# A pooled attention with two MLPs on one core: V rounded on GpSimd in the first batch, and new places in the planned order

## The chip, the cores and the metric

The kernel runs on one core of a Trainium2 chip. The core has a matrix engine (TensorE, PE in the rows; PEld is its weight load), VectorE (DVE), ScalarE (ACT), GpSimd (POOL) and SyncE (SP), which issues the DMAs here. The metric is the device time of one execution in microseconds. Three executions of the kernel before took 1319.75, 1320.28 and 1320.74 us; their median, 1320.28 us, is the time before.

## The reference

```python
q_pool = q.reshape(B, H, S // 2, 2, D).mean(axis=3)              # B, H, S, D = 4, 8, 1152, 64
scores = matmul(q_pool, k.transpose(0, 1, 3, 2)) / sqrt(D)
attn   = exp(scores - max(scores)); attn = attn / (sum(attn) + 1e-9)
x      = matmul(attn, v).transpose(0, 2, 1, 3).reshape(2304, 512)
h = x @ moe_w_in;   g = maximum(0.01 * h, h);                  x   = g @ moe_w_out     # 512 -> 2048 -> 512
h = x @ moe2_w_in;  g = where(h > 0, h, exp(min(h, 0)) - 1);   out = g @ moe2_w_out
```

q, k and v arrive in float32, the four weight matrices in float64.

## The kernel before

Every product on TensorE is made of two or three products of numbers that are split in a rounded high half and the rest (the low half). The helper `psplit` makes such a pair: one instruction rounds (a copy to the high half, mostly on ScalarE, L379), a second subtracts (the low half, mostly on GpSimd or VectorE, L386). K and V are split that way once for each head (`prep_k`, `prep_v`, L501 and L561); so are the probabilities after their transpose, and the weights after they have been converted from float64 (`convert`: two ScalarE instructions L411 and L413, two VectorE instructions L415 and L420 and one GpSimd addition L418 for every 256 columns).

The work is cut into 16 pairs of heads (four batches of four pairs). In a pair each of nine tiles of queries goes through the same steps: scores on TensorE (L585), maxima on VectorE (L590, L592), exponentials with row sums on ScalarE (L596), transposes of the probabilities (L637, from the tenth pair on by VectorE and DMA, L613), the split of the transposed tile `pt` (L379, L386), and the product P V (L668). The keys and queries of the second head of a pair are prepared while the first is worked on. When the four pairs of a batch are done, the two MLPs of the batch (up L820, down L854) run while the next batch's attention goes on, so TensorE always has two kinds of work; during the first batch there is no MLP to run. The last batch's MLPs, with the remaining rows of all batches, use a form with fewer products on 384 columns (`mlp_wide`, L1011 and L1073) and run after all attention has ended.

The order is not written by hand. Each step is recorded in `prog` with an engine, a cost and a rank, and `schedule` places the steps on each engine before the program is built: of the steps that are ready the one of lowest rank goes first. Ranks count in tiles (nine to a pair), and the table PLAN gives batch, layer, first rank, length in ranks and form of each MLP. LS, LR and LE are how many ranks ahead of its tile a step stands (scores, maxima, exponentials), PVLAG how many behind (P V), PREP where the second head's keys and queries stand against the pair. PATIENCE is the share of its own cost for which a step is held back when one of much lower rank is about to be ready; HOLD (in ns) is how long GpSimd holds back while VectorE, still busy, has a step waiting that uses the memory port shared by the two. On the chip every engine works off its own list in order and waits for what an instruction needs.

Of the kernel before, what the change touches and what calls it, by code (L numbers as in the profile page):

```python
# [9 lines left out]
F32 = mybir.dt.float32  # L10
# [37 lines left out]

class Program:

    PATIENCE = 0.5
    GAP = 16
    HOLD = 500
    HELD = 0
    BANKS = 8
    LATENCY = {"PE": 200, "SP": 3000, "DVE": 130, "DVE POOL": 200, "ACT": 155, "ACT POOL": 170, "POOL": 150,
# [195 lines left out]
def kernel(  # L252
# [26 lines left out]
    NP = H // 2  # L279
# [19 lines left out]
    WAHEAD = 1  # L299
    ACB = DC  # L300
    XFB = 5
    WH = "ACT"
    WL = "POOL"
    GH = "ACT"
    GL = "POOL"
# [17 lines left out]
    CAPS = (dict(s=4, t=4, o=1, h=2), dict(s=3, t=2, o=1, h=3), dict(s=3, t=2, o=1, h=7))  # L323
    T1B = 3
    WLAG = 1
    PLAN = ((0, 0, 34.0, 23.0, 0), (0, 1, 57.0, 23.0, 0), (1, 0, 80.0, 15.64, 0), (1, 1, 95.64, 15.64, 0), (2, 0, 111.28, 18.36, 0), (2, 1, 129.64, 18.36, 0), (3, 0, 148.0, 24.0, 1), (3, 1, 172.0, 24.0, 1))
    PBUF = 7
    DTB = 9
    DTC = (0, 1, 2)
    DTE = ("POOL", "POOL", "POOL")  # L330
    DTR = 0
# [2 lines left out]
    KKL = 0.5  # L334
    KH = 'ACT'
    ORDER = (0, 1, 2)
    LS = 2.5
    LR = 2
    LE = 0.3
    PVLAG = 0.5  # L340
    PREP = -1.5

    const = ctx.enter_context(tc.tile_pool(name="const", bufs=1))
    ident = const.tile([128, 128], F32, name="ident")
# [81 lines left out]
    def load_w(rank, layer, w_in, w_out, f, mine):  # L426

        src = (w_in[:, f * 128:(f + 1) * 128].rearrange("(c p) f -> p c f", p=128),
               w_out[f * 128:(f + 1) * 128, :])
        wi = mine("wi", [128, 2, DC, 128], F32R, WIB, "qT", KTB)  # L430
        wo = mine("wo", [128, 2, DM], F32R, WOB, "kT", KTB)
        both = lambda w: w.ap.rearrange("p a c n -> p (a c n)" if w is wi else "p a n -> p (a n)")
        flat = (lambda a: wi[:, a].rearrange("p c n -> p (c n)"), lambda a: wo[:, a])
        r = None
        for i, w in enumerate((wi, wo)):
            if (layer, f, i) in kept:
                kp = kept[layer, f, i]
                prog.add("SP", Move(128, 4096), rank - WAHEAD, lambda w=w, kp=kp: nc.sync.dma_start(
                    out=f32(both(w)), in_=kp.ap), w=[w], r=[kp])
                continue  # L440
            if r is None:
                r = sb("wr", [128, 1024], F32, WRB)
            o = 512 * i
            if w_in.dtype == F32:
                view = lambda o=o, i=i: r[:, o:o + 512].rearrange("p (c n) -> p c n", c=1 if i else DC)
                prog.add("SP", Move(128 if i else 512, 2048 if i else 512), rank - 1.5,
                         lambda i=i, view=view: nc.sync.dma_start(
                             out=view(), in_=src[i] if i == 0 else src[i].rearrange("p (c n) -> p c n", c=1)),
                         w=[(r, o), (r, o + 256)])
            else:  # L450
                convert(rank - CLEAD, r, src[i], o)
            psplit(rank - 0.5, WH, WL, lambda i=i: flat[i](0), lambda i=i: flat[i](1),
                   lambda o=o: r[:, o:o + 512], 512, (w, 0), [(r, o), (r, o + 256)], (w, 1))
            kp = kept[layer, f, i] = Buf(lambda i=i: dram.tile([128, 1024], F32, name=f"w{layer}_{f}_{i}"))
            prog.add("SP", Move(128, 4096), rank, lambda w=w, kp=kp: nc.sync.dma_start(
                out=kp.ap, in_=f32(both(w))), w=[kp], r=[w])
        return wi, wo
# [43 lines left out]
    def prep_k(rank, b, hp, j):  # L501
        kr = raw[b, hp, j, "k"]
        kn = sb("kn", [128, KC, 2 * D], F32R)
        psplit(rank, KH, "POOL", lambda: kn[:, :, 0:D], lambda: kn[:, :, D:2 * D], lambda: kr.ap,
               KC * D, (kn, "h"), [kr], fast=False)
        kT = sb("kT", [128, KC * 128], F32R, KTB)
        for c in range(3):
            t = tr_r(rank, kn, lambda i, c=c: kn[:, 3 * c + i, :], 3, [kT])
            prog.add("ACT", act(384), rank, lambda t=t, c=c: A.activation(  # L509
                out=kT[:, 384 * c:384 * c + 384].rearrange("p (c n) -> p c n", c=3),  # L510
                in_=f32(t[:, 0:3, :]), func=ACTF.Copy), w=[(kT, c)], r=[t])
        prep[b, hp, j, "k"] = kT
# [48 lines left out]
    def prep_v(rank, b, hp, j):  # L561
        vr = raw[b, hp, j, "v"]
        vn = sb("vn", [128, KC, 2 * D], F32R, KTB)
        o = D * j
        psplit(rank, KH, "POOL", lambda: vn[:, :, o:o + D], lambda: vn[:, :, D - o:2 * D - o],
               lambda: vr.ap, KC * D, (vn, "h"), [vr], fast=False)
        prep[b, hp, j, "v"] = vn

# [31 lines left out]
        return p  # L600

    def by_dma(b, hp):
        return b * NP + hp >= DTB

    def split_p(rank, b, hp, j, g, half, p, pt, c0):

        cs = DTC if by_dma(b, hp) else ()
        transpose_p(rank, p, [(pt, c0, 0, 128)], [c for c in ORDER if c not in cs], by_dma(b, hp))
        for c in cs:
            if not half:  # L610
                turned[j, g, c] = sb("wr", [128, 4, 3, 2, 32], F32, WRB, 1)
            tb = turned[j, g, c]
            prog.add("DVE", dve(384) + 60, rank, lambda c=c, tb=tb: V.transpose(  # L613
                out=tb[:, :, :, half, :].rearrange("p j k q -> p k j q"), in_=p[c].ap), w=[(tb, half)], r=[p[c]])
        if not half:
            return
        for c in cs:
            tb = turned[j, g, c]
            d = Buf(lambda c=c: dram.tile([4, 32, 4, 192], F32, name=f"p{b}_{hp}_{j}_{g}_{c}"))
            for i in range(4):  # L620
                prog.add("SP", Move(128, 768, 600), rank + DTR, lambda d=d, i=i, tb=tb: nc.sync.dma_start(
                    out=d.ap.rearrange("j a i r -> i a j r")[i],
                    in_=tb[32 * i:32 * i + 32].rearrange("a j k t q -> a j (k t q)")), w=[(d, i)], r=[tb])
            prog.add("SP", Move(128, 3072), rank + DTR, lambda c=c, d=d: nc.sync.dma_start(
                out=f32(pt[c][:, 1, 0:4]).rearrange("p i k r -> p (i k r)"),
                in_=d.ap.rearrange("j a i r -> (j a) (i r)")), w=[(pt[c], "d")], r=[d])
            psplit(rank + DTL, "ACT", DTE[c], lambda c=c: pt[c][:, 0, 0:4], lambda c=c: pt[c][:, 1, 0:4],
                   lambda c=c: f32(pt[c][:, 1, 0:4]), 3 * 256, (pt[c], ("h", 0)),
                   [(pt[c], "d")], (pt[c], ("l", 0)), fast=False)
# [145 lines left out]
    def mlp(at, span, blocks, layer, w_in, w_out, wide):  # L775
# [31 lines left out]
        def up(f):  # L807
# [5 lines left out]
            for hf, n in enumerate(cuts):  # L813
                h = hbank()
                t = mine("t1", [128, MAIN], F32, T1B, "raw", RAWB)
                tn, hn = lambda t=t, n=n: t[:, 0:n], lambda h=h, n=n: h[:, 0:n]

                def mm(h, c, n, hf):
                    for a, e in ((0, 0), (0, 1), (1, 0)):
                        PE.matmul(  # L820
                            out=h[:, 0:n], lhsT=wi[:, a, c, :], rhs=xs[hf][c][:, e],
                            start=(c == 0 and a == 0 and e == 0), stop=(c == DC - 1 and a == 1))

                for c in range(DC):
                    prog.add("PE", 3 * mmc(n), rank + step * hf / 2, lambda h=h, c=c, n=n, hf=hf: mm(h, c, n, hf),
                             w=[h], r=[wi, xs[hf][c]], want=[g[f][hf], t])
                rk = rank + step * hf / 2 - HURRY
                if layer == 0:
                    prog.add("ACT", act(n), rk, lambda tn=tn, hn=hn: A.activation(
                        out=tn(), in_=hn(), func=ACTF.Copy, scale=0.01), w=[t], r=[h])  # L830
                    prog.add("DVE", dve(n), rk, lambda tn=tn, hn=hn: V.tensor_tensor(
                        out=tn(), in0=hn(), in1=tn(), op=ALU.max), w=[t], r=[h, t])
                else:
                    prog.add("ACT", act(n), rk, lambda tn=tn, hn=hn: A.activation(
                        out=tn(), in_=hn(), func=ACTF.Exp), w=[t], r=[h])
                    prog.add("ACT", act(n, sbuf=True), rk, lambda tn=tn: A.activation(
                        out=tn(), in_=tn(), func=ACTF.Relu, bias=1.0, scale=-1.0), w=[t], r=[t])
                    prog.add("DVE", dve(n), rk, lambda tn=tn, hn=hn: V.scalar_tensor_tensor(  # L838
                        out=tn(), in0=tn(), scalar=-1.0, in1=hn(), op0=ALU.mult, op1=ALU.max),
                        w=[t], r=[h, t])  # L840
                psplit(rk, GH, GL, lambda gf=g[f][hf]: gf[:, 0], lambda gf=g[f][hf]: gf[:, 1], tn, n,
                       (g[f][hf], 0), [t], (g[f][hf], 1))

        def down(fc):
# [320 lines left out]
```

## Time and profile before

| | |
|---|---|
| median of three executions | 1320.28 us |
| the profiled execution, its time | 1319.28 us |
| its span, first to last instruction | 1317.2 us |
| busy: PE, DVE, ACT, POOL | 1272.9, 986.1, 925.6, 717.9 us |
| share of the span: PE, DVE, ACT, POOL | 97%, 75%, 70%, 55% |
| granted TensorE clock, mean | 0.999 |
| the chain that ended last | PE 78%, DVE 9%, ACT 8%, POOL 2%, DMA 2% |

The time of the profiled execution is 2.1 us longer than its span. The shares are means over three stretches that differ: attention alone (the first 150 us or so), attention beside MLPs (to about 1040 us), and the two wide MLPs. Matmuls overlap in the rows, so a TensorE that is shown busy may still run its matmuls further apart than they need to be.

### The profile page before, as it was taken

How to read it: one execution, taken by the hardware profiler on the slowest of the kernel's cores; microseconds unless marked ns; L12 is line 12 of the kernel's file. 1: busy time of each engine (PE TensorE's matmuls, PEld its weight loads, DVE VectorE, ACT ScalarE, POOL GpSimd, SP SyncE). 2: the span in 40 equal slices, each digit the busy share in tenths (PEclk: the TensorE clock that was granted, in tenths of full speed). 3: DMA queues.
4: the chain of work that ended last, by engine and by line, in shares of the span. 5: the costliest groups of instructions: out<-in, count | busy, mean ns of one | idle time of the engine just before them, and what ended most of it. 6: DMA issues, size and time to landing. Idle time of an engine off the chain costs nothing.

```text
span 1317.2 us, 22381 instructions
## 1 busy us (share of the span) xinstructions
PE 1272.9 (97%) x7016; PEld 1113.0 (84%) x7016; DVE 986.1 (75%) x2211; ACT 925.6 (70%) x2385; POOL 717.9 (55%) x633
## 2 busy tenths in 40 slices
PE   6998999999999999999999999999999999999998
PEld 5777878888878888888888888888888799998897
DVE  6999887888888989565665666666755677788876
ACT  8999989999899998665667666766675432226542
POOL 5344336776677765655566555665554464433530
PEclk9999999999999999999999999999999999999999
DMA  6343425666656657998898979988988444443331
GB/s 189 117 152 124 148 65 187 208 224 207 216 197 234 224 203 252 328 286 291 258 301 283 307 242 320 318 286 289 284 272 275 170 145 138 135 144 113 136 119 49
DMA packets 145653, 277.78 MB, mean 211 GB/s; under 512 B 15744, under 2 KB 77184, under 8 KB 145536
## 3 DMA queue, kind: packets, MB, share of 16 engines
q1 hardware_dynamic: 145536, 276.36, 64.2%
q8 instruction: 56, 0.92, 0.3%
q14 instruction: 61, 0.50, 0.1%
HBM read 195.56 MB, written 71.30 MB: 203 GB/s over the span
## 4 chain that ended last, share of the span: by engine, by line
PE 78%; DVE 9%; ACT 8%; POOL 2%; DMA 2%; issue 1%; SPq 0%; DVEq 0%; POOLq 0%; ACTq 0%
PE b L854 18%; PE b L820 17%; PE b L1073 10%; PE b L668 10%; PE b L585 9%; PE b L1011 8%; PE b L637 4%; DVE pt L386 2%; ACT p L596 2%; DVE m L590 2%; ACT pt L379 2%; DMA pt<-p 1%; PE b L496 1%; DVE wr L420 1%; ACT kT L509 1%
## 5 line engine op out<-in xcount | busy, mean ns | idle before, releaser
L820 PE MATMUL b<-xs,wi 128*128 128x512 f32 x1152 | 322.2, 402 | 3.1 <-DVE t L838 1.3
L596 ACT ACTIVATE p<-b,m 128x384 f32<-128x384 f32 x432 | 250.6, 592 | 43.5 <-DVE m L592 42.5
L590 DVE TENSOR_REDUCE m<-b 128x1 f32<-128x384 f32 x432 | 230.4, 550 | 58.0 <-PE b L585 54.6
L820 PEld LDWEIGHTS b<-xs,wi 128*128 128x128 f32 x1152 | 205.2, 188 | 37.7 <-DVE t L838 2.0
L585 PE MATMUL b<-kT,qT 128*128 128x384 f32 x768 | 193.2, 350 | 6.9 <-ACT p L596 3.3
L386 POOL TENSOR_TENSOR pt<-pt 128x768 fp32r<-128x768 f32 x84 | 155.1, 1851 | 78.5 <-ACT pt L379 58.9
L668 PE MATMUL b<-pt,vn 128*128 128x256 f32 (+1 forms) x1152 | 191.3, 301 | 5.1 <-DVE pt L386 1.7
L668 PEld LDWEIGHTS b<-pt,vn 128*128 128x128 f32 x1152 | 171.2, 189 | 19.9 <-DVE pt L386 4.9
L386 POOL TENSOR_TENSOR g<-t,g 128x512 fp32r<-128x512 f32 x96 | 125.1, 1305 | 103.1 <-ACT g L379 79.7
L386 DVE TENSOR_TENSOR pt<-b,pt 128x384 fp32r<-128x384 f32 (+1 forms) x312 | 143.7, 489 | 30.2 <-ACT pt L379 27.8
L854 PE MATMUL b<-g,wo 128*128 128x512 f32 x576 | 160.6, 402 | 0.9 <-DVE qT L530 0.8
L585 PEld LDWEIGHTS b<-kT,qT 128*128 128x128 f32 x768 | 132.6, 190 | 26.1 <-ACT p L596 6.3
L854 PE MATMUL b<-wo,g 128*128 128x512 f32 x576 | 154.5, 399 | 0.0
L379 ACT ACTIVATE pt<-b 128x384 fp32r<-128x384 f32 (+1 forms) x312 | 127.4, 451 | 25.6 <-PE b L637 24.7
L418 POOL TENSOR_TENSOR wr<-wr,ct 128x256 uint32<-128x256 uint32 x128 | 93.7, 739 | 68.0 <-DVE wr L415 33.5
L637 PE MATMUL b<-ident,p 128*128 128x128 f32 x792 | 121.9, 275 | 6.5 <-DVE t L838 1.7
L854 PEld LDWEIGHTS b<-wo,g 128*128 128x128 f32 x576 | 104.8, 188 | 18.6
L637 PEld LDWEIGHTS b<-ident,p 128*128 128x128 f32 x792 | 95.9, 141 | 28.1 <-ACT p L596 4.8
L854 PEld LDWEIGHTS b<-g,wo 128*128 128x128 f32 x576 | 102.8, 188 | 17.9 <-DVE qT L530 1.1
L613 DVE STREAM_TRANSPOSE wr<-p 128x384 f32<-128x384 f32 x168 | 91.6, 564 | 31.1 <-ACT p L596 15.7
L596 ACT ACTIVATION_READ_ACCUMULATOR p<-b,m 128x1 f32 x432 | 93.4, 216 | 0.0
L379 ACT ACTIVATE pt<-pt 128x768 fp32r<-128x768 f32 (+1 forms) x88 | 72.9, 830 | 20.7 <-DMA pt<-p 18.1
(180 smaller groups left out, 2307.7 us busy)
## 6 DMA issues: line engine op xcount, KB each, us to landing
wi<-w SPq DMA_DIRECT2D x96, 512.0 KB, 4.9
wo<-w SPq DMA_DIRECT2D x96, 512.0 KB, 4.9
p<-wr SPq DMA_DIRECT2D x336, 96.0 KB, 3.8
pt<-p SPq DMA_DIRECT2D x84, 384.0 KB, 5.4
cr<-in_moe_w_in_dram SPq DMA_DIRECT2D x64, 256.0 KB, 3.0
cr<-in_moe_w_out_dram SPq DMA_DIRECT2D x64, 256.0 KB, 3.1
w<-wi SPq DMA_DIRECT2D x32, 512.0 KB, 3.7
w<-wo SPq DMA_DIRECT2D x32, 512.0 KB, 3.6
```

The costliest lines, as they stand in the source:

```text
L379: prog.add("ACT", act(n, sbuf=not psum), rank, lambda: A.activation(out=hi(), in_=src(), func=ACTF.Copy), w=[w], r=r)
L386: lambda: eng.tensor_tensor(out=lo(), in0=src(), in1=f32(hi()), op=ALU.subtract),
L418: prog.add("POOL", pool(CW), rank, lambda t=t, to=to: G.tensor_tensor(out=to(), in0=to(), in1=t.ap, op=ALU.add), w=part, r=[t] + part)
L585: PE.matmul(out=st[:, 0:384], lhsT=qa(), rhs=kT[:, 384 * c:384 * c + 384], start=(i == 0), stop=(i == len(seq) - 1))
L590: prog.add("DVE", dve(384), rank - LR, lambda st=st, c=c: V.tensor_reduce(out=m[:, c:c + 1], in_=st[:, 0:384], axis=AX.X, op=ALU.max), w=[ ...
L596: prog.add("ACT", act(384, True), rank - LE, lambda c=c: A.activation(out=p[c].ap, in_=banks[c][:, 0:384], func=ACTF.Exp, bias=m[:, 3:4], ...
L637: PE.transpose(out=t[:, i, :], in_=p[c][:, 128 * i:128 * i + 128], identity=ident)
L668: PE.matmul(out=o[:, 0:n], lhsT=vn[:, c, :], rhs=pt[th][:, a, :, c % 3, :] if by_dma(b, hp) else pt[th][:, a, c % 3, :], start=(c == 3 * O ...
L820: PE.matmul(out=h[:, 0:n], lhsT=wi[:, a, c, :], rhs=xs[hf][c][:, e], start=(c == 0 and a == 0 and e == 0), stop=(c == DC - 1 and a == 1))
L854: PE.matmul(out=y[:, 0:n], lhsT=g[f][hf][:, e, part] if layer else w[f][1][:, a, part], rhs=w[f][1][:, a] if layer else g[f][hf][:, e], st ...
L1011: PE.matmul(out=bk[:, 0:NH], lhsT=get(a, i), rhs=xv(e), start=i == 0 and a == 0 and e == 0, stop=i == 1 and a == 1)
L1073: PE.matmul(out=y[:, 0:n], lhsT=g[f][hf][:, e, part] if layer else w[f][1][:, a, part], rhs=w[f][1][:, a] if layer else g[f][hf][:, e], st ...
```

## The change

- The rounding of V (the high half in `prep_v`) is given to GpSimd in batch 0, eight instructions; it was on ScalarE. In the other batches it stays there. No other instruction changes its engine, and none is added or dropped: of 8050 steps these eight differ.
- Ranks: scores LS 2.5 to 3, maxima LR 2 to 3, P V PVLAG 0.5 to 1.2, second head's keys and queries PREP -1.5 to -0.5.
- PLAN: the MLPs of batch 1 get 16.5 ranks each (15.64 before), those of batch 2 16.5 (18.36 before), and the wide MLPs start at rank 146 (148 before).
- `schedule`: PATIENCE 0.5 to 0.8, HOLD 500 to 800.
- Knobs at their old values: WH as a pair of ScalarE, KHF and KH1 (K), GH0 (the first MLP's high half) and DTA (early pairs by DMA, empty).

```diff
-    PATIENCE = 0.5
+    PATIENCE = 0.8
-    HOLD = 500
+    HOLD = 800
...
-    PLAN = ((0, 0, 34.0, 23.0, 0), (0, 1, 57.0, 23.0, 0), (1, 0, 80.0, 15.64, 0), (1, 1, 95.64, 15.64, 0), (2, 0, 111.28, 18.36, 0), (2, 1, 129.64, 18.36, 0), (3, 0, 148.0, 24.0, 1), (3, 1, 172.0, 24.0, 1))
+    PLAN = ((0, 0, 34, 23, 0), (0, 1, 57, 23, 0), (1, 0, 80, 16.5, 0), (1, 1, 96.5, 16.5, 0), (2, 0, 113.0, 16.5, 0), (2, 1, 129.5, 16.5, 0), (3, 0, 146.0, 24, 1), (3, 1, 170.0, 24, 1))
...
-    LS = 2.5
-    LR = 2
+    LS = 3
+    LR = 3
     LE = 0.3
-    PVLAG = 0.5
-    PREP = -1.5
+    PVLAG = 1.2
+    PREP = -0.5
...
+    VHF = 'POOL'
...
     def prep_v(rank, b, hp, j):
-        psplit(rank, KH, "POOL", lambda: vn[:, :, o:o + D], lambda: vn[:, :, D - o:2 * D - o],
+        psplit(rank, VHF if b == 0 else KH, "POOL", lambda: vn[:, :, o:o + D], lambda: vn[:, :, D - o:2 * D - o],
                lambda: vr.ap, KC * D, (vn, "h"), [vr], fast=False)
```

The first place is ScalarE's list at the start of the first pair (`vn` is V split in halves, `kT` the transposed keys, `p` the probabilities, `pt` their transposed tile). Before:

```order
L509 ACTIVATE kT<-b_181 128x384
L509 ACTIVATE kT<-b_185 128x384
L379 ACTIVATE vn<-raw 128x9x64
L509 ACTIVATE kT<-b_191 128x384
L528 ACTIVATE qT<-b_203 128x512
L596 ACTIVATE p,sum<-b_157,m 128x384
L596 ACTIVATE p,sum<-b_166,m 128x384
L596 ACTIVATE p,sum<-b_175,m 128x384
L379 ACTIVATE pt<-b_242 128x3x128
L379 ACTIVATE vn<-raw 128x9x64
L379 ACTIVATE pt<-b_261 128x3x128
```

And now (line numbers are five or six higher):

```order
L514 ACTIVATE kT<-b_184 128x384
L514 ACTIVATE kT<-b_189 128x384
L514 ACTIVATE kT<-b_195 128x384
L601 ACTIVATE p,sum<-b_157,m 128x384
L533 ACTIVATE qT<-b_206 128x512
L601 ACTIVATE p,sum<-b_166,m 128x384
L601 ACTIVATE p,sum<-b_175,m 128x384
L384 ACTIVATE pt<-b_227 128x3x128
L384 ACTIVATE pt<-b_247 128x3x128
L384 ACTIVATE pt<-b_255 128x3x128
```

Both roundings of V have left the list, and the exponentials stand behind three copies and no longer behind five instructions.

The second place is GpSimd's list at the same time (`wr` is a weight under conversion, `qn` and `qxn` pooled queries). Before, and then now:

```order
L518 TENSOR_TENSOR qn<-raw 128x512
L418 TENSOR_TENSOR wr<-wr,ct 128x256
L543 TENSOR_TENSOR qxn<-qrem 128x128
L386 TENSOR_TENSOR vn<-raw,vn 128x9x64
L543 TENSOR_TENSOR qxn<-qrem 128x128
L418 TENSOR_TENSOR wr<-wr,ct 128x256
L386 TENSOR_TENSOR vn<-raw,vn 128x9x64
```

```order
L523 TENSOR_TENSOR qn<-raw 128x512
L387 CAST vn<-raw 128x9x64
L391 TENSOR_TENSOR vn<-raw,vn 128x9x64
L387 CAST vn<-raw 128x9x64
L391 TENSOR_TENSOR vn<-raw,vn 128x9x64
L548 TENSOR_TENSOR qxn<-qrem 128x128
L423 TENSOR_TENSOR wr<-wr,ct 128x256
```

Each V now takes two GpSimd instructions in a row, and the first weight additions stand behind them.

The third place is TensorE's list where the ninth pair's first P V stands (`xs` is the MLP's input, `wi` and `wo` its weights, `pt,vn` the operands of P V). Before:

```order
L637 MATMUL b_6989<-ident,p 128x128 x3
L820 MATMUL b_6948<-xs,wi 128x512 x3
L585 MATMUL b_7005<-kT,qT 128x384 x2
L637 MATMUL b_7013<-ident,p 128x128 x3
L637 MATMUL b_7028<-ident,p 128x128 x3
L637 MATMUL b_7039<-ident,p 128x128 x3
L668 MATMUL b_7046<-pt,vn 128x256 x6
L637 MATMUL b_7059<-ident,p 128x128 x3
L637 MATMUL b_7068<-ident,p 128x128 x3
L668 MATMUL b_7046<-pt,vn 128x256 x6
```

And now:

```order
L643 MATMUL b_6947<-ident,p 128x128 x3
L826 MATMUL b_6956<-xs,wi 128x512 x9
L643 MATMUL b_6983<-ident,p 128x128 x3
L826 MATMUL b_6956<-xs,wi 128x512 x3
L590 MATMUL b_7000<-kT,qT 128x384 x2
L643 MATMUL b_7003<-ident,p 128x128 x3
L590 MATMUL b_7014<-kT,qT 128x384 x2
L643 MATMUL b_7018<-ident,p 128x128 x3
L674 MATMUL b_7025<-pt,vn 128x256 x6
L643 MATMUL b_7047<-ident,p 128x128 x3
L674 MATMUL b_7025<-pt,vn 128x256 x6
```

The transposes are no longer bunched right ahead of the product: MLP matmuls and scores stand between them.

## Rows read from the trace of the kernel before

**Rows 1.** The page: span, busy time by engine.

```profile
span 1317.2 us, 22381 instructions
...
PE 1272.9 (97%) x7016; PEld 1113.0 (84%) x7016; DVE 986.1 (75%) x2211; ACT 925.6 (70%) x2385; POOL 717.9 (55%) x633
```

**Rows 2.** Busy time by stretch; the first line names the columns.

```profile
core 0: us, PE busy (x) PEld busy (x) DVE busy (x) ACT busy (x) POOL busy (x), PEclk, DMA share, GB/s
0.00:150.00 150.00, 127.91 (x846) 109.71 (x846) 130.46 (x335) 141.97 (x416) 65.81 (x71) 1.00 0.48 146
150.00:200.00 50.00, 46.84 (x290) 40.59 (x291) 40.52 (x99) 42.85 (x123) 20.49 (x18) 1.00 0.29 86
...
200.00:500.00 300.00, 294.26 (x1695) 254.12 (x1694) 254.15 (x612) 281.32 (x772) 211.93 (x211) 0.99 0.65 213
```

**Rows 3.** Instruction groups of ScalarE, 0 to 150 us: busy, mean ns, idle before.

```profile
L509 ACT ACTIVATE kT<-b 128x384 fp32r<-128x384 f32 x24 | 11.3, 512 | 3.9 <-PE b L496 3.8
L411 ACT ACTIVATE cm<-cr 128x256 f32<-128x256 f32 x24 | 11.3, 469 | 0.0
...
L379 ACT ACTIVATE kn<-raw 128x576 fp32r<-128x576 f32 x8 | 5.6, 695 | 1.5 <-DMA raw<-in_k_dram 1.5
L379 ACT ACTIVATE vn<-raw 128x576 fp32r<-128x576 f32 x8 | 5.4, 680 | 0.0
```

**Rows 4.** Timeline of ScalarE at three places: start us, us, instruction.

```profile
12.57 0.68 ACT L379 ACTIVATE vn<-raw 128x576 fp32r<-128x576 f32 x1
13.14 0.48 ACT L509 ACTIVATE kT<-b 128x384 fp32r<-128x384 f32 x1
...
168.02 0.61 ACT L596 ACTIVATE p<-b,m 128x384 f32<-128x384 f32 x1
...
457.89 0.43 ACT L413 ACTIVATE ct<-cr 128x256 uint32<-128x256 uint32 x1
458.22 0.63 ACT L379 ACTIVATE wo<-wr 128x512 fp32r<-128x512 f32 x1
458.74 0.62 ACT L379 ACTIVATE g<-t 128x512 fp32r<-128x512 f32 x1
```

**Rows 5.** The chain of waits in order of time: start us, us, what.

```profile
103.31 1.54 PE b L668 x12
...
197.49 2.10 PE b L820 x9
```

**Rows 6.** VectorE, 0 to 150 us: groups, then line L415 (ns min/median/max).

```profile
L590 DVE TENSOR_REDUCE m<-b 128x1 f32<-128x384 f32 x97 | 52.2, 551 | 6.2 <-PE b L585 5.0
L386 DVE TENSOR_TENSOR pt<-b,pt 128x384 fp32r<-128x384 f32 x83 | 43.1, 550 | 1.0 <-ACT pt L379 0.2
...
L415 DVE TENSOR_SCALAR wr<-cm 128x256 uint32<-128x256 uint32 x22 | 8.2, 383 | 0.3
...
L415 DVE TENSOR_SCALAR wr<-cm x22: 284/290/952, 9.8 to 137.1; 128x256 uint32<-128x256 uint32 x22
```

**Rows 7.** The split of V on GpSimd, 0 to 150 us.

```profile
L386 POOL TENSOR_TENSOR vn<-raw,vn 128x576 fp32r<-128x576 f32 x8 | 11.3, 1417 | 8.4 <-ACT vn L379 5.5 <-ACT qT L528 1.6 <-DVE wr L420 1.3
```

**Rows 8.** Waits of TensorE from 200 us on: us in total, times, longest.

```profile
PE b L1011 <- DVE pt L386: 2.7, 3, 1.5
PE b L637 <- DVE t L838: 1.7, 1, 1.7
PE b L668 <- ACT pt L379: 1.5, 1, 1.5
...
PE b L668 <- POOL pt L386: 0.7, 2, 0.4
...
PE b L668 <- DVE pt L386: 0.4, 1, 0.4
...
PE b L585 <- ACT kT L509: 0.3, 1, 0.3
```

**Rows 9.** Ten microseconds around the longest wait before P V, columns of group 2.

```profile
460.00:470.00 10.00, 8.04 (x46) 7.18 (x45) 8.56 (x19) 8.92 (x24) 6.92 (x8) 0.83 0.54 184
```

More of the change, by code (lines that the diff above doesn't have):

```diff
@@ L301 @@
     XFB = 5
-    WH = "ACT"
+    WH = ("ACT", "ACT")
     WL = "POOL"
@@ L325 @@
     WLAG = 1
-    PLAN = ((0, 0, 34.0, 23.0, 0), (0, 1, 57.0, 23.0, 0), (1, 0, 80.0, 15.64, 0), (1, 1, 95.64, 15.64, 0), (2, 0, 111.28, 18.36, 0), (2, 1, 129.64, 18.36, 0), (3, 0, 148.0, 24.0, 1), (3, 1, 172.0, 24.0, 1))
+    PLAN = ((0, 0, 34, 23, 0), (0, 1, 57, 23, 0), (1, 0, 80, 16.5, 0), (1, 1, 96.5, 16.5, 0), (2, 0, 113.0, 16.5, 0), (2, 1, 129.5, 16.5, 0), (3, 0, 146.0, 24, 1), (3, 1, 170.0, 24, 1))
     PBUF = 7
     DTB = 9
+    DTA = {}
+    KHF = 'ACT'
+    VHF = 'POOL'
+    KH1 = 'ACT'
+    GH0 = 'ACT'
     DTC = (0, 1, 2)
@@ L451, in load_w @@
                 convert(rank - CLEAD, r, src[i], o)
-            psplit(rank - 0.5, WH, WL, lambda i=i: flat[i](0), lambda i=i: flat[i](1),
+            psplit(rank - 0.5, WH[i], WL, lambda i=i: flat[i](0), lambda i=i: flat[i](1),
                    lambda o=o: r[:, o:o + 512], 512, (w, 0), [(r, o), (r, o + 256)], (w, 1))
@@ L503, in prep_k @@
         kn = sb("kn", [128, KC, 2 * D], F32R)
-        psplit(rank, KH, "POOL", lambda: kn[:, :, 0:D], lambda: kn[:, :, D:2 * D], lambda: kr.ap,
+        psplit(rank, KHF if b == 0 else KH1 if b == 1 else KH, "POOL", lambda: kn[:, :, 0:D], lambda: kn[:, :, D:2 * D], lambda: kr.ap,
                KC * D, (kn, "h"), [kr], fast=False)
@@ L602, in by_dma @@
     def by_dma(b, hp):
-        return b * NP + hp >= DTB
+        return b * NP + hp >= DTB or b * NP + hp in DTA
     def split_p(rank, b, hp, j, g, half, p, pt, c0):
-        cs = DTC if by_dma(b, hp) else ()
+        early = b * NP + hp < DTB
+        cs = (DTA.get(b * NP + hp, ()) if early else DTC)
         transpose_p(rank, p, [(pt, c0, 0, 128)], [c for c in ORDER if c not in cs], by_dma(b, hp))
@@ L610, in split_p @@
             if not half:
-                turned[j, g, c] = sb("wr", [128, 4, 3, 2, 32], F32, WRB, 1)
+                turned[j, g, c] = sb("wr", [128, 4, 3, 2, 32], F32, WRB, -1 if early else 1)
             tb = turned[j, g, c]
@@ L840, in up @@
                         w=[t], r=[h, t])
-                psplit(rk, GH, GL, lambda gf=g[f][hf]: gf[:, 0], lambda gf=g[f][hf]: gf[:, 1], tn, n,
+                psplit(rk, GH0 if at < 60 else GH, GL, lambda gf=g[f][hf]: gf[:, 0], lambda gf=g[f][hf]: gf[:, 1], tn, n,
                        (g[f][hf], 0), [t], (g[f][hf], 1))
```

## The prediction

> **What bounds the kernel now.** I read the page first, then the busy time by stretch, then the groups and waits of the stretch that stood out. By the page TensorE is busy 97% of the span [rows 1], which looks like a kernel with nothing to win but fewer matmuls, and the change drops none. The stretches say otherwise. In the first 150 us, where only attention runs, ScalarE is busy 141.97 us, VectorE 130.46, TensorE 127.91 [rows 2]. Nearly all the rest that ScalarE has there lies in its first microseconds: the groups of that stretch show idle time before the first copies of the keys (3.8 us until the first transposes, 1.5 us for a load) and none before the conversions or the roundings of V [rows 3]. So ScalarE sets the pace there, and TensorE waits for it in small pieces. From 200 to 500 us TensorE is busy 294.26 of 300 us and ScalarE 281.32 [rows 2]: TensorE is the bound, ScalarE stands close behind. What the change can win is therefore TensorE's lost time in the first stretch; what it can lose is new waits after it.
>
> To put the loss on the bound engine's own scale I added, along each engine's list, the undisturbed distance from one start to the next. For matmuls that is 2.10/9 = 0.233 us for 512 columns and 1.54/12 = 0.128 us for P V [rows 5], for ScalarE 13.14 - 12.57 = 0.57 us for a rounding of V, 0.33 us for one conversion, 0.52 us for a weight rounding [rows 4] (a group's mean, 0.680 us for V [rows 3], holds the overlap with the next instruction too, so it is not the saving). At each product I took what ScalarE must have issued before it less what TensorE has issued before it. That difference is a lead which TensorE cannot avoid waiting for. Its largest value before is 28.7 us, at a P V of the fourth pair; VectorE's largest is 15.2 us.
>
> **The change part by part.**
>
> *V's rounding in batch 0.* Eight ScalarE instructions of 0.57 us [rows 4] leave the bound engine: 8 x 0.57 = 4.6 us off the path. GpSimd gets eight more. No row shows this copy on GpSimd. From above it is the subtraction of the same size, 1.417 us with two inputs [rows 7], from below ScalarE's 0.57; I take 1.4. That is 11 us on an engine that is busy 65.81 of 150 us [rows 2], so its own time is covered. V is wanted only at P V, and with PVLAG later still. Price if the cover fails: below, as a rival.
>
> *ScalarE's list.* The higher ranks of scores and maxima bring exponentials forward and push weight conversions back. Ahead of the last exponential of batch 0, which started at 168.02 us [rows 4], stand 26 + 26 conversions and ten weight roundings before, and 17 + 17 and seven now, besides the eight V. That is 18 x 0.33 + 3 x 0.52 = 7.5 us less. It is moved, not removed, so only part counts: by the same sums the largest lead over TensorE falls from 28.7 to 20.0 us and moves behind batch 0, to a transpose of the fifth pair. Of these 8.7 us, 4.6 are V; the order gives 4.1. Its lower bound is nothing (the conversions come due when TensorE needs the weights), its upper bound the whole 7.5. VectorE is next: its largest lead becomes 13.1 us, still below ScalarE's, so I let the full 8.7 count.
>
> *P V later, MLP matmuls between transposes and P V.* After 200 us TensorE waits 1.5 + 0.7 + 0.4 = 2.6 us before P V [rows 8], and around the longest of these its granted clock was 0.83 over 10 us [rows 9], some 1.7 us more. In the new list the transposes are spread out there. Against that stands that every place is new, and a new list can have its own such place. The bounds are -4.3 and +4.3 us; I take -1.0.
>
> *Second head's keys and queries one rank later; PLAN.* TensorE's waits for copied keys are 0.3 us from 200 us on [rows 8], so there is little to win and slack to spend: 0. The table's new ranks shift MLP work between stretches in which TensorE is bound anyway. Where the wide MLP's first products stand, TensorE's list has the same work ahead of them to within 7 us of matmuls. Its waits there, 2.7 us [rows 8], bound this on both sides; I take 0.
>
> *GpSimd yields longer.* This moves GpSimd's steps, which nothing on the path waits for in the first stretch; 0, bounded by the 2.0 us that the port costs today. That figure is VectorE's line L415: mean 383 ns, median 290, 22 times, so 22 x 0.093 = 2.0 us [rows 6]. GpSimd's 11 us more make that 2.0 x 11/66 = 0.3 us longer; I take +0.4.
>
> The sum, on the profiled execution's 1319.3 us: -4.6 - 4.1 - 1.0 + 0.4 = -9.3, so 1310.0. The median of the runs stands 1.0 us above that execution, so **1311 us**. Next late in the first stretch are VectorE (130.46 us of work in some 141) and ScalarE again.
>
> Here a rule speaks against the first step. Row L415 shows one VectorE instruction take from 284 to 952 ns [rows 6]. The Trainium skill (SBUF — State Buffer, Who interferes with whom) says that VectorE and GpSimd share a pair of ports as an exclusive lock, so that a VectorE instruction in a two-port mode, or with two SBUF inputs, stands still for a whole GpSimd instruction. The long L415 agree with it. By that rule alone up to eight roundings would be added to VectorE; without it, nothing.
>
> **The rivals.**
>
> *Only V's share stays.* The conversions that were pushed back fall due just when batch 0's MLP starts, on a ScalarE that is 94% busy to 500 us [rows 2]. For it: the lead stays near 20 us in my sums until the sixth pair. Against: ScalarE rests 18.7 us in that stretch. The gain is then 4.6 us: 1319.3 - 4.6 + 1.0 = 1315.7.
>
> *VectorE pays for GpSimd.* Each rounding of up to 1.42 us [rows 7] stands against a VectorE instruction that needs the port, and VectorE is behind anyway: 8 x 1.42 = 11.4 us, 130.46 + 11.4 = 141.8, as much as ScalarE has today. Nothing is won: 1320. For it: L415's spread. Against: the bulk of VectorE's work here, maxima and pt, keeps to 550 ns [rows 6], and reads PSUM.
>
> *Later keys hold up the second head (slower).* At the second head of each of 16 pairs, TensorE's list comes to the scores before the last copy of that head's keys is there. The chain is 0.7 us of rounding, 1.4 of subtraction and three copies of 0.5 [rows 3, 7], with three transposes about 4.2 us; it was started a rank earlier (168/36 = 4.7 us in the first batch). If a quarter of it is bare in every pair, that is 16 x 1.05 = 17 us: 1311 + 17 = 1328. It decides from the point where the last copy ends after everything ahead on TensorE's list. Against: 2.5 ranks are left between preparation and scores, and the 0.3 us above.
>
> *More is won.* All waits before P V, the clock's 1.7 us and the 1.7 us wait of a transpose for an MLP's maximum [rows 8] go: 2.6 + 1.7 + 1.7 - 1.0 = 5 us more, 1306.
>
> **How the numbers follow.** The forecast has 0.52 (its own range 1307 to 1315), only V's share 0.16, VectorE pays 0.10, later keys 0.10, more 0.12. Below 0.2% (2.6 us) a measurement of this kernel cannot be told from no change. Faster: the forecast, "more" and most of "only V" make 0.77; the same: most of "VectorE pays" and a rest of "only V", 0.10; slower: later keys and the upper end of "VectorE pays", 0.13. The range 1304 to 1320 leaves out later keys, half of "VectorE pays" and a little below.
>
> **What would show it.** Right: in the first 150 us TensorE's busy time goes up by some 6 us; the last exponential of batch 0 starts 9 to 12 us before 168; ScalarE is still over 92% busy there; line L415 keeps its median, with a few more long ones. Wrong: VectorE's groups in that stretch have longer means (the port); ScalarE stays full past 500 us and TensorE waits for weights or g (given back); waits of scores for kT in the list of TensorE's waits, or a lower granted clock in some stretch between 200 and 1025 us (new waits).

## The result and the profile after

The changed kernel takes 1309.15 us (median of six executions, 1308.12 to 1313.01) against 1320.55 us of six of the kernel before: ratio 0.9917, interval 0.9904 to 0.9930. The forecast was 1311. The profiled execution took 1309.90 us with a span of 1308.1 us, 9.1 us less than the one shown before.

On the page of the changed kernel TensorE's busy time is a few us less than in [rows 1] and its share the same, so the page does not tell where the time went:

```profile
PE 1266.6 (97%) x7016; PEld 1112.9 (85%) x7016; DVE 980.0 (75%) x2211; ACT 920.3 (70%) x2377; POOL 721.8 (55%) x641
```

Three stretches of the changed kernel, columns as in [rows 2]:

```profile
0.00:150.00 150.00, 133.67 (x907) 119.28 (x907) 132.39 (x344) 141.53 (x425) 63.96 (x71) 1.00 0.41 125
...
200.00:500.00 300.00, 293.55 (x1702) 253.66 (x1700) 254.44 (x615) 280.95 (x766) 212.74 (x211) 1.00 0.66 219
500.00:1025.00 525.00, 517.75 (x2691) 443.82 (x2690) 328.09 (x730) 336.68 (x800) 297.51 (x198) 1.00 0.86 282
```

And the last of the three in the kernel before:

```profile
500.00:1025.00 525.00, 520.88 (x2720) 446.98 (x2719) 336.92 (x745) 344.58 (x823) 301.00 (x202) 1.00 0.88 287
```

In the first 150 us TensorE is busy 5.8 us longer (133.67 against 127.91) and has started 907 matmuls, not 846. From 500 to 1025 us it is busy a little less (517.75 against 520.88). The last exponential of batch 0 starts 12.4 us sooner than in [rows 4]; this is the timeline of ScalarE:

```profile
155.58 0.62 ACT L601 ACTIVATE p<-b,m 128x384 f32<-128x384 f32 x1
```

On GpSimd the split of V is now two instructions; groups of 0 to 200 us:

```profile
L391 POOL TENSOR_TENSOR vn<-raw,vn 128x576 fp32r<-128x576 f32 x10 | 14.2, 1423 | 9.6 <-DVE tm L708 3.7 <-PE b L643 2.4 <-DMA cr<-in_moe_w_out_dram 1.9
...
L387 POOL CAST vn<-raw 128x576 fp32r<-128x576 f32 x8 | 5.3, 665 | 8.4 <-PE b L674 6.7 <-PE b L590 1.8
```

And VectorE from 0 to 150 us, to set against [rows 6]: the maxima, the halves of pt, the conversion L420 (L415 before) and that line's shortest, median and longest.

```profile
L595 DVE TENSOR_REDUCE m<-b 128x1 f32<-128x384 f32 x106 | 55.7, 550 | 4.9 <-PE b L590 3.8
L391 DVE TENSOR_TENSOR pt<-b,pt 128x384 fp32r<-128x384 f32 x86 | 44.8, 548 | 0.9 <-ACT pt L384 0.3
...
L420 DVE TENSOR_SCALAR wr<-cm x16: 234/284/755, 9.8 to 146.2; 128x256 uint32<-128x256 uint32 x16
```

The means have not moved, so VectorE does not pay for the eight casts.

The experiments of the next section are put beside the two kernels in one table. "Lost" is, as in the prediction, what TensorE's starts lie further apart than the undisturbed spacing of their matmuls, summed over a stretch of the profiled execution; TensorE's work by that measure is 1225.8 us in each of them. "Lead" is the prediction's largest lead of ScalarE over TensorE, summed over the lists. "Dips" counts how often in the profiled execution the granted clock fell to the lower of its two levels (1.2 instead of 2.4 GHz), leaving out the first 20 us and the fall at the end; what that costs is part of "lost". Ratios are against the kernel before timed beside the same version; it took 1320.55 us beside the changed kernel and 1321.50 to 1321.99 beside the others, so versions are compared by their ratios and not by their medians.

| kernel | median us | ratio, interval | last exp. of batch 0 | lost 0-200 | 200-500 | 500-1025 | later | lead | dips |
|---|---|---|---|---|---|---|---|---|---|
| before | 1320.55 | 1 | 168.0 | 44.1 | 15.5 | 13.0 | 7.9 | 28.7 | 1 |
| changed | 1309.15 | 0.9917, 0.9904-0.9930 | 155.6 | 33.2 | 16.1 | 16.1 | 5.7 | 20.0 | 0 |
| f1: old order, V on GpSimd | 1323.10 | 1.0016, 1.0004-1.0027 | 168.6 | 44.4 | 16.7 | 13.1 | 7.9 | 24.1 | 2 |
| g1: old order, short maxima | 1320.01 | 0.9995, 0.9984-1.0007 | 167.3 | 43.3 | 16.8 | 14.3 | 8.9 | | 3 |
| g2: both | 1319.27 | 0.9987, 0.9978-0.9997 | 167.9 | 43.9 | 16.8 | 16.2 | 7.9 | | 3 |
| f2: new order, V on ScalarE | 1313.86 | 0.9939, 0.9921-0.9958 | 159.3 | 36.8 | 17.6 | 15.2 | 6.1 | 24.6 | 1 |
| a1: V alone, new plan | 1316.96 | 0.9971, 0.9960-0.9982 | 161.3 | 36.8 | 21.6 | 13.0 | 6.7 | 22.5 | 2 |
| b1: all but V | 1318.06 | 0.9977, 0.9967-0.9987 | 159.5 | 37.3 | 17.5 | 15.8 | 5.7 | 23.4 | 0 |
| a2: ranks alone | 1319.03 | 0.9983, 0.9973-0.9993 | 160.8 | 37.2 | 16.6 | 17.8 | 8.9 | 25.2 | 1 |
| c1: scores, maxima alone | 1329.86 | 1.0059, 1.0045-1.0074 | 163.7 | 38.8 | 23.8 | 18.7 | 9.7 | 26.6 | 4, one twice as long |
| c2: later P V alone | 1320.25 | 0.9987, 0.9977-0.9996 | 164.0 | 40.0 | 18.4 | 15.5 | 7.3 | 28.1 | 1 |
| b5: changed, old PLAN | 1318.22 | 0.9976, 0.9964-0.9988 | 155.5 | 32.9 | 17.4 | 23.0 | 7.3 | 20.0 | 3 |
| b4: changed, old PATIENCE, HOLD | 1312.72 | 0.9932, 0.9918-0.9947 | 155.3 | 32.8 | 19.9 | 17.2 | 6.8 | 19.9 | 2 |
| b3: changed, K on GpSimd too | 1313.73 | 0.9943, 0.9930-0.9956 | 157.1 | 33.5 | 17.6 | 19.0 | 5.7 | 14.8 | 3 |

By it the change won 10.9 us in the first 200 us and gave 1.5 back later. The clock hides a part of that. A dip costs TensorE about 1.5 us: f2's starts are 3.65 us later than those of the changed kernel ahead of f2's dip at 412 us, and 5.1 us later past it. The profiled execution of the kernel before had one dip, at 463 us [rows 9], and that of the changed kernel none, so without the clock about 3 us were given back and not 1.5.

The clock differs between the executions of one kernel too. Take off each time the share by which its mean granted clock lies below 1; the medians are then 1317.1 to 1317.6 us for the three sets of the kernel before that were timed beside the experiments, 1306.4 for the changed kernel, 1316.5 for f1, 1310.7 for f2, 1312.3 for b5 and 1310.1 for b4. Below, "without the clock" means these estimates. The clocks are given to three digits, so they are good to about 0.7 us.

### The profile page after: what moved, and what is told of

Read it like the earlier page. It is cut to its first block, busy times and chain, and to the rows that moved or that the text cites. A ratio compares the mean times of both kernels' runs of the same rounds, so it can differ in the third digit from the quotient of the medians.

```text
span 1308.1 us, 22407 instructions
## 1 busy us (share of the span) xinstructions
PE 1266.6 (97%) x7016; PEld 1112.9 (85%) x7016; DVE 980.0 (75%) x2211; ACT 920.3 (70%) x2377; POOL 721.8 (55%) x641
## 4 chain that ended last, share of the span: by engine, by line
PE 68%; ACT 12%; DVE 11%; DMA 4%; issue 2%; POOL 1%; SPq 1%; ACTq 0%; DVEq 0%; POOLq 0%
PE b L860 16%; PE b L826 14%; PE b L1079 10%; PE b L1017 8%; PE b L590 8%; PE b L674 7%; ACT pt L384 3%; ACT p L601 3%; PE b L643 3%; DVE pt L391 3%; DVE m L595 2%; DMA pt<-p 2%; DMA p<-wr 1%; DVE wr L425 1%; ACT cm L416 1%
## 5 line engine op out<-in xcount | busy, mean ns | idle before, releaser
L826 PE MATMUL b<-xs,wi 128*128 128x512 f32 x1152 | 317.3, 400 | 1.2 <-DVE t L844 0.6
L674 PE MATMUL b<-pt,vn 128*128 128x256 f32 (+1 forms) x1152 | 193.0, 302 | 6.5 <-DVE pt L391 2.6
L674 PEld LDWEIGHTS b<-pt,vn 128*128 128x128 f32 x1152 | 168.0, 189 | 19.4 <-DVE pt L391 5.4
L590 PEld LDWEIGHTS b<-kT,qT 128*128 128x128 f32 x768 | 134.3, 190 | 28.7 <-ACT p L601 2.9
L384 ACT ACTIVATE pt<-b 128x384 fp32r<-128x384 f32 (+1 forms) x312 | 128.1, 450 | 20.4 <-PE b L643 18.7
L860 PEld LDWEIGHTS b<-wo,g 128*128 128x128 f32 x576 | 103.7, 188 | 16.8
L860 PEld LDWEIGHTS b<-g,wo 128*128 128x128 f32 x576 | 102.9, 188 | 16.6 <-DVE pt L391 1.1
```

Source lines behind the costliest of these rows:

```text
L384: prog.add("ACT", act(n, sbuf=not psum), rank, lambda: A.activation(out=hi(), in_=src(), func=ACTF.Copy), w=[w], r=r)
L590: PE.matmul(out=st[:, 0:384], lhsT=qa(), rhs=kT[:, 384 * c:384 * c + 384], start=(i == 0), stop=(i == len(seq) - 1))
L674: PE.matmul(out=o[:, 0:n], lhsT=vn[:, c, :], rhs=pt[th][:, a, :, c % 3, :] if by_dma(b, hp) else pt[th][:, a, c % 3, :], start=(c == 3 * O ...
L826: PE.matmul(out=h[:, 0:n], lhsT=wi[:, a, c, :], rhs=xs[hf][c][:, e], start=(c == 0 and a == 0 and e == 0), stop=(c == DC - 1 and a == 1))
L860: PE.matmul(out=y[:, 0:n], lhsT=g[f][hf][:, e, part] if layer else w[f][1][:, a, part], rhs=w[f][1][:, a] if layer else g[f][hf][:, e], st ...
```

## The experiments

**f1, the eight roundings alone, nothing else moved.** The step is placed as ScalarE's and issued on GpSimd, so every list keeps its order but for the eight instructions.

```diff
+        if b == 0:
+            prog.add("ACT", act(KC * D, sbuf=True), rank, lambda: G.tensor_copy(out=vn[:, :, o:o + D], in_=vr.ap),
+                     w=[(vn, "h")], r=[vr])
...
```

> The order of before is kept, instruction for instruction, and only the eight roundings of V of batch 0 are issued on GpSimd instead of ScalarE. ScalarE sets the pace of the first stretch: 8 x 0.57 = 4.6 us faster than before (3 to 5.5). VectorE sets it, or pays for GpSimd: no gain, within 1.5 us. New places alone made the gain: no gain.

No gain: 1323.10 us, if anything 0.16% slower, and the clock makes that difference (without it 1316.5 us against 1317.1). ScalarE and the rest from 0 to 150 us:

```profile
0.00:150.00 150.00, 127.37 (x844) 110.18 (x845) 129.76 (x334) 137.64 (x406) 70.65 (x79) 1.00 0.49 147
```

ScalarE has 4.3 us less to do and rests 4.3 us more; TensorE does not start one matmul more. The timeline of ScalarE shows where the first V went. In [rows 4] it began at 12.57, between copies of the keys; here the list is the same without it:

```profile
12.04 1.26 ACT L509 ACTIVATE kT<-b 128x384 fp32r<-128x384 f32 x3 [1.58 <-PE b L496]
14.41 0.60 ACT L528 ACTIVATE qT<-b 128x512 fp32r<-128x512 f32 x1 [1.12 <-PE b L524]
```

The next copy waits 1.12 us for transposes on TensorE. About half of that, 0.55 us, is a wait that the rounding had filled and that its removal uncovered. The other half is the clock of this execution: the transposes ahead of the copy start 0.213 us apart here and 0.109 in the kernel before, so TensorE was still at the lower level. By 15 us TensorE is 0.8 us behind the kernel before, 0.2 of that from its first matmul on; at 110 us it is 0.8 behind as well, and from 200 to 360 us 0.5. So in this order the eight roundings were worth 0.3 us to it, and 0.6 by the medians without the clock. What ScalarE gained by them it waits elsewhere: from 15 to 150 us its waits, without the one shown, are 3.9 us here and 0.8 before, 2.2 and 0.6 of them for transposes ahead of pt. A list that is full because a planner filled its gaps looks like the list of a bound engine.

**f2, the opposite: the new order, V back on ScalarE at the same places.**

```diff
+        if b == 0:
+            prog.add("POOL", pool(KC * D), rank, lambda: A.activation(out=vn[:, :, o:o + D], in_=vr.ap, func=ACTF.Copy),
+                     w=[(vn, "h")], r=[vr])
...
```

> The order of the changed kernel is kept, and the eight roundings of V of batch 0 go back to ScalarE at the same places. ScalarE sets the pace: 4.6 us slower than the changed kernel, about 1314, 6 to 7 us faster than before. New places alone made the gain: as the changed kernel, 1309.

1313.86 us, 2.9 us slower than the changed kernel by the ratios (0.9939 - 0.9917, on 1320; the intervals overlap a little), 4.3 without the clock. TensorE loses 3.6 us more in the first 200 us, and in the profiled executions its starts fall behind step by step, 1.4 us by 50 us, 2.8 by 100, 3.7 by 150. So in the new order the eight roundings cost 3 to 4 us, most of the 4.6 that were worked out, at the places which the planner had chosen for GpSimd. The chain of waits from 15 to 165 us fits that. Its shares by line, of the kernel before, of f2 and of the changed kernel (that of f1 is much like the first):

```profile
by line: PE b L668 15.3%; PE b L585 11.8%; DVE pt L386 11.8%; ACT p L596 11.3%; ACT pt L379 10.2%; DVE m L590 9.0%; PE b L637 3.8%; ACT kT L509 3.4%; issue 2.7%; PE b L820 2.3%; ACT tm L676 2.2%; ACT vn L379 1.9%; PE b L496 1.7%; ACT qT L52
```

```profile
by line: ACT p L608 22.2%; ACT pt L384 15.8%; PE b L597 9.8%; PE b L681 8.7%; PE b L650 5.5%; DVE pt L391 5.1%; issue 3.7%; DVE m L602 3.3%; ACT tm L689 3.3%; ACT kT L514 3.1%; ACT vn L571 2.9%; ACT kn L384 2.4%; ACT ct L418 2.2%; ACT qT L5
```

```profile
by line: ACT p L601 15.1%; ACT pt L384 13.0%; PE b L590 12.9%; PE b L674 10.2%; DVE pt L391 7.5%; DVE m L595 7.2%; PE b L643 6.4%; issue 3.5%; ACT kT L514 3.2%; ACT kn L384 2.5%; ACT tm L682 2.2%; ACT ct L418 2.0%; ACT cm L416 1.7%; ACT qT 
```

Before, P V, scores, pt on two engines, exponentials and maxima have 9 to 15% each: three engines take turns. In the new order with V on ScalarE exponentials and pt on ScalarE lead with 38%, and with V on GpSimd they have 28%. The shares are a hint and no proof, as g2 will show.

**a1 and b1, V alone and all but V, planned anew.**

```diff
-        psplit(rank, KH, "POOL",        # a1, on the kernel before
+        psplit(rank, "POOL" if b == 0 else KH, "POOL",
...
-    VHF = 'POOL'                        # b1, on the changed kernel
+    VHF = 'ACT'
```

> Before, with V's rounding of batch 0 on GpSimd and the order planned anew for it; ranks, PLAN, PATIENCE and HOLD as before. ScalarE sets the pace: 4.6 us faster than before, give or take 2 us that a new order brings. VectorE pays: no gain.

> The changed kernel with V's rounding of batch 0 on ScalarE, planned anew. The sum of the prediction has 4.1 + 1.0 us for the order: about 5 us faster than before, 1315. V alone made the gain: no gain against before. New places alone: 1309.

V alone with a new plan: ratio 0.9971, 3.8 us, as expected; all but V: 0.9977, 3.0 us where 5 were expected. a1 against f1 is the plan alone: V on GpSimd in both, 7.6 us less lost in the first 200 us, 4.9 of it lost again from 200 to 500 us. The product of the two ratios, 0.9948, is above the 0.9917 of both together, by more than the intervals. Either the parts help each other or the planner found a lucky order for the whole: each version that is planned anew is one order only, and c1 below shows that a new order can cost 0.6%. These runs do not separate the two.

**g1 and g2, less work on VectorE in the old order.** In batch 0 the maximum is taken over 256 of 384 columns of each bank; any shift leaves the softmax as it is.

```diff
-                out=m[:, c:c + 1], in_=st[:, 0:384], axis=AX.X, op=ALU.max), w=[(m, c)], r=[st])
+                out=m[:, c:c + 1], in_=st[:, 0:256 if b == 0 else 384], axis=AX.X, op=ALU.max), w=[(m, c)], r=[st])
```

> The order of before, nothing moved; in batch 0 each of the 108 maxima reads 256 of its 384 scores (any shift gives the same softmax), which takes about 128 x 1.05 ns = 0.13 us each, 14.5 us in all, off VectorE alone. If the three engines hold each other up in turn (the chain of before from 15 to 165 us spends 9.0% of 150 us = 13.5 us on these maxima, some 30% of them): about 4 us faster than before. If ScalarE alone sets the pace: no gain. If VectorE alone: 9 us or more.

> The last one, and V's eight roundings of batch 0 on GpSimd at the same places. If V was worth nothing in the old order because VectorE held ScalarE up, V counts now: 3 to 4.6 us faster than g1. If V's rounding is worth nothing there for another reason (GpSimd's list, TensorE's): as g1.

Neither does much: 0.9995 (the interval holds 1 and ends at a gain of 2.1 us) and 0.9987. The maxima did get shorter as expected, 420 ns for 552. From 0 to 150 us of g2, VectorE and ScalarE are both less busy than in [rows 2], by 9.5 and 4.1 us, and TensorE is about where it was:

```profile
0.00:150.00 150.00, 129.01 (x847) 112.02 (x848) 120.93 (x335) 137.87 (x408) 70.78 (x79) 0.99 0.48 146
```

A dip of the granted clock at 113 us, in this one execution, took back 1.3 us of TensorE's start times. Ahead of it they are 0.7 us before those of g1, which is about what V is worth here; by the ratios it is 1 us. The chain of g1 has even more ScalarE than that of f2:

```profile
by line: ACT p L596 25.7%; ACT pt L379 17.5%; PE b L668 9.2%; PE b L585 6.7%; ACT kT L509 4.8%; issue 4.4%; DVE pt L386 4.3%; ACT cm L411 2.9%; ACT tm L676 2.7%; PE b L637 2.4%; PE b L820 2.3%; ACT vn L379 2.3%; ACT ct L413 2.3%; ACT qT L52
```

and V off ScalarE should then have counted in full. Instead ScalarE waits for transposes; its waits from 15 to 150 us, g1 and then g2:

```profile
ACT pt L379 <- PE b L637: 0.4, 1, 0.4
```

```profile
ACT pt L379 <- PE b L644: 3.3, 7, 1.2
```

All rivals that I wrote down for g1 but "ScalarE alone" fall with g1, and that one falls with f1. So no single engine's amount of work set the pace in the old order. Which loop of waits did (scores wait for a bank that the exponentials release, transposes for the exponentials, ScalarE's copies for the transposes) is not settled by these runs.

**a2, c1, c2, the ranks.**

```diff
+    LS = 3        # a2, c1
+    LR = 3        # a2, c1
+    PVLAG = 1.2   # a2, c2
+    PREP = -0.5   # a2
```

> Before with the ranks of the changed kernel alone (LS, LR, PVLAG, PREP), planned anew; PLAN, PATIENCE, HOLD and V as before. If the ranks are what freed ScalarE: 3 us faster than before, as the kernel with all but V. If PLAN or PATIENCE and HOLD did: no gain.

> Before with LS 3 and LR 3 alone, planned anew. The ranks together ended the first batch's exponentials earlier, by the trace. If scores and maxima did it (more tiles under way, so that ScalarE and VectorE do not wait for each other's turn): the last exponential of batch 0 starts 7 to 10 us before 168.0, and the time is 2 to 5 us below before. If it was P V: within 2 us of 168.0, and no gain.

> Before with PVLAG 1.2 alone, planned anew. If P V right behind its transposes is what held TensorE's list up: the last exponential of batch 0 starts 7 to 10 us before 168.0, and the time is 2 to 5 us below before. If scores and maxima did it: within 2 us of 168.0, and no gain.

Each frees the first stretch: 6.9, 5.3 and 4.1 us less lost to 200 us, the last exponential 4 to 7 us sooner. None keeps it. a2 ends 0.17% ahead, c2 0.13%, and c1 is 0.59% slower than before: 8.3 us more lost from 200 to 500 and 5.7 from 500 to 1025. Both expectations for c1 and c2 missed: each had one of the two as the cause, with 7 to 10 us for the last exponential and 2 to 5 us of time, or nothing. It is both, in part. PREP alone was not run.

**b5 and b4, the changed kernel with the old PLAN, or the old PATIENCE and HOLD.**

```diff
+    PLAN = ((0, 0, 34.0, 23.0, 0), (0, 1, 57.0, 23.0, 0), (1, 0, 80.0, 15.64, 0), (1, 1, 95.64, 15.64, 0), (2, 0, 111.28, 18.36, 0), (2, 1, 129.64, 18.36, 0), (3, 0, 148.0, 24.0, 1), (3, 1, 172.0, 24.0, 1))   # b5
...
+    PATIENCE = 0.5   # b4
+    HOLD = 500       # b4
```

> The changed kernel with the old PLAN, planned anew. TensorE is bound where PLAN moves work: as the changed kernel, 1309 to 1311, if the prediction's 0 for PLAN holds; 3 us or more slower if PLAN keeps the gain of the first batch from being given back later.

> The changed kernel with the old PATIENCE 0.5 and HOLD 500, planned anew. If the prediction's 0 for them holds: 1309 to 1311, as the changed kernel. If they are part of the gain: 2 us or more slower.

The old PLAN costs 7.8 us of the gain (0.9976 against 0.9917, intervals apart), and 5.9 without the clock. The first 200 us are untouched, 32.9 lost; from 500 to 1025 us 23.0 are lost, not 16.1. TensorE's waits from 500 to 1110 us in b5:

```profile
PE b L674 <- POOL pt L391: 5.6, 3, 2.6
PE b L590 <- DMA kn<-kT: 1.7, 1, 1.7
```

and the same two in the changed kernel:

```profile
PE b L590 <- DMA kn<-kT: 0.7, 1, 0.7
PE b L674 <- POOL pt L391: 0.6, 1, 0.6
```

The last pairs' probabilities go by VectorE, DMA, ScalarE and GpSimd before P V can use them, and with the old PLAN TensorE comes to those products too soon. Its lists show it for two of the three waits, which stand in the fifteenth pair: between the last P V of the fourteenth pair and that of the fifteenth there are 129 MLP matmuls in b5, 192 in the changed kernel and 174 in the kernel before, and the pair takes 59 us in b5 and 69 in the changed kernel. The longest wait, 2.6 us at 1024 us, stands in the last pair, where the counts are 225 and 216; its cause is not shown. The stretch from 900 to 1000 us, b5 first, then the changed kernel:

```profile
900.00:1000.00 100.00, 94.79 (x475) 81.29 (x474) 61.88 (x141) 66.08 (x157) 53.60 (x35) 0.97 0.83 269
```

```profile
900.00:1000.00 100.00, 99.56 (x511) 85.52 (x510) 63.73 (x142) 66.64 (x160) 53.57 (x35) 1.00 0.83 267
```

In b5 the granted clock is 0.97 there, two dips to the lower of its two levels: at 910 us, behind waits of TensorE of 0.4 and 1.5 us that end at 908 and 910, and at 951 us, behind waits of 1.5 and 1.7 us that end at 948 and 951. They make some 3 us of the 6.9 that b5 loses more from 500 to 1025 us. The new PLAN with the old ranks was not run, so what PLAN is worth by itself is open. PATIENCE and HOLD are worth 2.0 us by the ratios, with intervals that overlap, and 3.7 without the clock: likely, not shown; the two were not separated.

**b3, K on GpSimd as well.**

```diff
-    KHF = 'ACT'
+    KHF = 'POOL'
```

> The changed kernel with K's rounding of batch 0 on GpSimd as well, eight more instructions of 0.58 us off ScalarE, planned anew. If ScalarE still sets the pace: up to 4.6 us faster than the changed kernel, about 1305. If the three engines now hold each other up (its chain is 62 us of 135 on ScalarE from 15 to 150 us): about 2 us. GpSimd is late with the keys: slower than the changed kernel.

1313.73 us, slower than the changed kernel (0.9943 against 0.9917). The lead falls by 5 us and the first 200 us lose as much as in the changed kernel, 33.5 against 33.2, so eight more roundings off ScalarE win nothing there; why is not shown. 4.4 us more are lost between 200 and 1025 us, with three dips of the clock. No version tried beats the changed kernel.

## Why the prediction came out, point by point

Two of the points rest on TensorE's waits from 200 us on in the changed kernel (the keys' transposes L501, P V L674):

```profile
PE b L501 <- POOL kn L391: 2.4, 1, 2.4
...
PE b L674 <- DVE pt L391: 1.8, 4, 0.8
...
PE b L674 <- ACT pt L384: 1.5, 2, 1.0
```

- *The stretch.* Right. The gain is in the first 200 us, 10.9 us by the loss of TensorE, where 8.7 were forecast; the last exponential came at 155.6, inside the "9 to 12 us before 168" but for 0.4. VectorE's means did not rise.
- *"Eight ScalarE instructions leave the bound engine: 4.6 us off the path."* This step failed as put. In the old order the same eight are worth 1 us at most (f1, g2), in the new order 3 to 4 us (f2). ScalarE was full, but not alone the bound. The split between V and the order was off with it: in the profiled executions, of the 10.9 us in the first 200 us, V has 3.6, where 4.6 were forecast, and the order 7.3, where 4.1 were (44.1 before, 36.8 in f2, 33.2 in the changed kernel).
- *The lead.* It is a floor under the loss, and I used its fall as the fall of the loss. It fell by 8.7, and the loss by 10.9. In f1 it fell by 4.6 and in b3 by 5.2, and the loss by nothing in either. In the kernel before 28.7 of 44.1 us are lead, and the other 15 are waits that the sums over the lists leave out; f1, g1 and g2 show that less work on ScalarE or VectorE does not shorten the loss by itself.
- *The copy on GpSimd.* Cost taken as 1.4 us, measured 0.665 [row of the cast above]; it was covered either way, and that GpSimd holds VectorE up hardly showed (L420 at most 755 ns; in f1, with the old order, the mean of L415 rose from 383 to 408 ns, 22 x 0.025 = 0.6 us, near the 0.4 of the sum). The Trainium skill (GPSIMD Engine Reference, Engine selection) has two-input operations on GpSimd about twice as slow as on VectorE, and one-input ones at roughly line rate. The traces agree: in the kernel before, a two-input instruction on 128x512 takes 1305 ns on GpSimd (L386, g) and 686 on VectorE (L831, which reads one input from a bank), and the cast's 665 ns are less than half of the subtraction's 1423.
- *P V later: -1.0.* From 200 us on the waits before P V grew from 2.6 us [rows 8] to 1.8 + 1.5 + 0.6 = 3.9. The dip that stood there in the kernel before is gone in the profiled execution, but the loss after 200 us grew by 1.5 us in all. Within the bounds given, on the wrong side.
- *Keys one rank later: 0.* The longest wait after 200 us is now one for keys, 2.4 us at 671 us, where GpSimd comes late to a low half of K. The kernel before has no such wait from 200 us on, and neither has the profiled execution of f2, whose lists differ from these in the eight roundings alone. So the rival of later keys shows, in one place and not in 16; whether PREP makes it is not shown. That nothing on the path waits for GpSimd in the first stretch was misread too: the first transposes of keys wait for its low half 5.7 us, in both kernels.
- *PLAN: 0.* Wrong by 7.8 us, beyond its bound of 2.7. I took TensorE to be bound wherever PLAN moves work. It is, as long as enough MLP matmuls stand between the last pairs' steps, and PLAN sets how many do (129 against 192 in the fifteenth pair). The rivals had the new waits, but priced them for late keys and not for P V of the last pairs. PATIENCE and HOLD at about 0: 2 us, within doubt.
- *The sign "given back".* It hardly came in the whole change (1.5 us, or about 3 without the clock), and it came in most parts of it: a1, a2, c1, c2 and b5 win in the first 200 us and lose 5 to 16 us more than before after them. So it was in part luck that the sum came out: a gain taken 2 us too small in the first stretch stood beside a later loss of 1.5 us that was put at a gain of 1.0. The sum, which had PLAN at 0, also forecasts b5, the change without its new PLAN: 9.3 us, where b5 gains 3.2.

## What to carry to other kernels

Where a planner fills idle time, an engine that is busy 98% of a stretch (ScalarE here from 15 to 150 us) is no proof of a bound, and a chain that names it most is only a hint: expect little from taking work off it unless the order is made anew, and separate the two by an experiment that keeps the order, as f1 and f2 do. When a stage is won, look at once at what a table of the later stages (here PLAN) was fitted to: a1, a2, c1, c2 and b5 won 4 to 11 us in the first stretch and lost 5 to 16 more than before after it, and the whole kept most of what it won.

## What was not expected of the hardware

GpSimd rounds 128 x 576 float32 in 662 to 672 ns, as fast as ScalarE does (680), and less than half of its own subtraction of that size. Taking 9 us of busy time off VectorE and 4 off ScalarE over 150 us moved almost nothing: with the lists unchanged, starts on TensorE between 200 and 360 us lay within 0.8 us of the kernel before in f1, g1 and g2.
